# A gated mix of two linear attentions on one core: the output weights' splitting copies get one place in each half iteration, behind the copies of K and V

## The chip, the cores and the metric

The kernel runs on one core of a Trainium2 chip. The metric is the device time of one execution in microseconds (us); the median of three runs counts. A profile of one execution gives the times of single instructions.

## The reference

Two attention blocks A and B work on the same input x of 2048 tokens by 448 features, with 16 heads of 28, and a gate mixes their outputs. Each block projects x to q, k and v, sends q and k through a matrix per head and through two softmaxes (of the result and of its negative), and attends linearly: a sum of phi_k^T V over all tokens, read by phi_q and divided by a denominator. All of it is fp32.

```python
def block(x, wqkv, w_phi, wo):                 # once for A, once for B
    qkv = (x @ wqkv).reshape(B, S, 3, H, Dh).transpose(2, 0, 3, 1, 4)
    q, k, v = qkv[0], qkv[1], qkv[2]
    pq = einsum("bhsd,hdf->bhsf", q, w_phi)
    pk = einsum("bhsd,hdf->bhsf", k, w_phi)
    phi_q = concatenate([softmax(pq), softmax(-pq)], -1)
    phi_k = concatenate([softmax(pk), softmax(-pk)], -1)
    kv = einsum("bhsf,bhsd->bhfd", phi_k, v)
    z = einsum("bhsf->bhf", phi_k)
    num = einsum("bhqf,bhfd->bhqd", phi_q, kv)
    den = einsum("bhqf,bhf->bhq", phi_q, z)[..., None] + 1e-6
    return (num / den).transpose(0, 2, 1, 3).reshape(B, S, D) @ wo
g = sigmoid((x * gate_w).sum(-1, keepdims=True))
out = g * block_A(x) + (1 - g) * block_B(x)
```

## The kernel before

**Tiles.** The 2048 tokens are 16 tiles of 128. Each tile has three projections on TensorE: K and Q (weights already multiplied with the feature matrices, in `rk` and `rq`) and V (`rv`). Every fp32 operand is split in two: a *high part* (a copy to the rounded type fp32r, on ScalarE, `ACT`) and a *low part* (the rest, a subtraction on GpSimd, `POOL`, or VectorE, `DVE`). A projection of a tile and block is then 11 matmuls into one PSUM bank: `K0`, `K1` for K, `Q`, and `VA`, `VB` or `O0` for V. Inside the main loop 10 of them come together, and the last ones of K, Q and V are gathered in `halves` (L449 in the profile).

**A half iteration.** The loop `for p in range(2, 6)` in `steps()` has two halves, i = 0 and 1, of about 13 to 14 us each. A half projects K of tile k, Q of tile q = k - 2 and V, and takes these results onward. ScalarE copies V out of its banks (rows `vs<-VA`, `vs<-VB`, `vs<-O`) and K out of its two (`pk<-K`, twice). VectorE takes maxima and minima of K (`mx`), GpSimd subtracts them, ScalarE makes the exponentials (`ret<-ret`), VectorE sums them (`sm`), and GpSimd normalises (`ret<-ret,sm`). Q goes the same way on a longer road: VectorE reads the bank (`qmx`, `ru`), a transfer to DRAM and back turns it (`qd<-ru`, then `ru<-qd`), and behind that come two more exponentials (`ret<-ru`, `ret<-ret 128x32x28`). At every second half, TensorE accumulates phi_k^T V of two tiles into bank `T0` (`kv`, L535).

**The output weights.** They come as 7 chunks of 128 rows. `wo_rows` brings them into the right row order in DRAM (`wos`). `split_wo(c)` does one chunk: a load into the staging buffer (`wst<-wos`, 224 KB), the high part on ScalarE, the low part on GpSimd, and a store of each (`wod<-wst`). There is one staging buffer: the load of a chunk can begin only when the low part of the chunk before has read it, and the high part's own buffer is free when its store is done. `load_wo` brings all chunks into `rk`, when the last K projection has read it (`rk<-wod`, twice 1.6 MB). The output projection uses them from about 248 us on (L672).

**What sets the order.** Each step is put in by `plan.add(engine, cost, function, reads, writes)` (`put` adds with a cost by size). Reads and writes are names such as `("ws", 0)`, the staging buffer, or `("pk", 0, b)`, the K copy of an even tile, and give the dependences. `Plan.order` then runs a list scheduler over the steps with these costs: TensorE keeps the order of `steps()`, on every other engine the ready step with the earliest due time goes first. Each engine executes its queue in the order that comes out, and waits for semaphores at the head of it.

`split_wo` is called from `steps()` by `"wo", c`: chunk 0 in the loop at p = 2, chunks 1 and 6 both at p = 3, i = 0, chunk 2 at p = 4, chunk 3 at p = 5, chunks 4 and 5 behind the loop. In the loop a list `behind` already exists, with the names of the copies of K and of V of this half; it is given to `S`, the first softmax part of Q, whose exponential so comes behind these copies.

Of the kernel before, what the change touches and what calls it, by code (L numbers as in the profile page):

```python
# [108 lines left out]
def steps():  # L109

    yield from (("V01", 0, 0, 1), ("x1",), ("V01", 1, 0), ("V01", 1, 1), ("wt", 0), ("wt", 1), ("x", 2), ("wt", 2), ("wt", 3), ("V", 2, 0), ("F", 0, "DP"), ("V", 2, 1))
    yield from (("V", 3, 0), ("F", 1, "NP"), ("V", 3, 1), ("F", 2, "DP"), ("V", 4, 0), ("F", 3, "DP"), ("x2",), ("later",), ("V", 4, 1), ("k", 0, 0), ("q", 0, 0), ("k", 0, 1), ("ks", 0))
    yield from (("K", 1), ("wo_rows",), ("q", 0, 1), ("qf", 0))
    yield from (("S", 0, JIT % 3 - 1), ("K", 2), ("Q", 1), ("S", 1, (JIT - 1) % 3 - 1), ("k", 3, 0), ("k", 3, 1), ("vm", 5, 0), ("kv", 0, 1), ("vo", 5, 0), ("ks", 3), ("V", 5, 1))
    for p in range(2, 6):
        yield "x", p + 1
        for i in range(2):
            k, q, v = 2 * p + i, 2 * p - 2 + i, 2 * p + 1 + i
            yield "k10", k
            yield "q10", q  # L120
            yield "halves", k, q, v if v >= 6 else None
            if i:
                yield "kv", q - 1, q
            yield "ks", k
            yield "qf", q
            if v >= 6:
                yield "vo", v, 0
                yield "vo", v, 1
            behind = [("pk", k % 2, b) for b in range(2)] + [("v", v % NV, b) for b in range(2) if v >= 6]
            if q > 2:  # L130
                yield "S", q - 1, (JIT - q + 1) % 3 - 1, behind
            if i == 0:
                yield "wo", p - 2
                if p == 3:
                    yield "wo", 6
            yield "v10" if k < 11 else "V", v + 1
    yield from (("x", 7), ("K", 12), ("S", 9, 0, [("pk", 0, b) for b in range(2)]), ("Q", 10), ("turn", JIT - 2, 1), ("turn", JIT - 1, 0), ("wo", 4), ("k", 13, 0), ("k", 13, 1), ("kv", 10, 11), ("ks", 13), ("Q", 11), ("gates", 0, 12), ("gates_b", 0, 12))
    yield from (("K", 14), ("V", 14, 0), ("k", 15, 0), ("k", 15, 1), ("kv", 12, 13), ("wo", 5), ("load_wo",), ("Q", 12), ("ks", 15), ("V", 14, 1), ("V", 15, 0), ("q", 13, 0), ("q", 13, 1))
    yield from (("V", 15, 1), ("free_v",), ("free_k",), ("kv", 14, 15), ("free_e",), ("fetch", 0, 2), ("fetch", 1, 3))
    yield from (("kv_turn",), ("gates", 12, NT), ("qf", 13), ("Q", 14))  # L140
    kept, late = list(range(2, JIT - 2)), list(range(JIT, NT))
    rest = []
    while kept or late:
        rest.append((kept.pop(0) if kept else late.pop(0), late.pop(0) if late else kept.pop(0)))
    pairs = [((JIT - 1, JIT - 2), (0, 1)), ((0, 1), (2, 3))] + [(t, (2 * (i % 2), 2 * (i % 2) + 1)) for i, t in enumerate(rest)]
    for p, (tiles, slots) in enumerate(pairs):
        yield "num", tiles, slots
        if p == 0:
            yield from (("Q", 15), ("free_x",), ("free_q",))
        if p:  # L150
            for i, t in enumerate(pairs[p - 1][0]):
                yield "out", 2 * p - 2 + i, t, ("O0", "O1")[i]
        end = p == len(pairs) - 1
        yield "mix", p, ("DVE", "DVE") if end else ("POOL", "POOL"), ("T0", "T1"), ("DVE", "DVE") if end else ("POOL", "POOL")
        if p == 1:
            yield "gates_b", 12, NT, [("o", 2)]
        if p + 2 < len(pairs):
            for t, s in zip(*pairs[p + 2]):
                yield ("S" if t >= JIT else "fetch"), t, s, *([[("qd", 14, 3)]] if t == 2 else [[("ob", 0)]] if t == 3 else [])
    for i, t in enumerate(pairs[-1][0]):  # L160
        yield "out", 2 * len(pairs) - 2 + i, t, ("O0", "O1")[i]


JIT = 10
# [4 lines left out]
def hedgehog_mix(ctx: ExitStack, tc: tile.TileContext, xd, wv, wkt, wqt, wphi, wo, cmask, cpmask, out):  # L169
# [106 lines left out]
    def put(eng, n, fn, r, w, **k):  # L276
        add(eng, both(eng, n), fn, r, w, **k)
# [120 lines left out]
                add("SP", 0.4, dma(wos[:, i:i + n, c].rearrange("g i n -> i g n"), r[lo - DH * k:lo - DH * k + n]), [("q", "l", 1, 1, 2)], [("wos", c, i)], lat=3, kb=16 * n)  # L398
                lo += n

    def split_wo(c):
        s = [wst[:, i] for i in range(3)]
        f = [wst.bitcast(F32R)[:, i] for i in range(3)]
        add("SP", 0.4, dma(s[0], wos[:, :, c].rearrange("g i n -> (g i) n")), [k for k in plan.writer if k[:2] == ("wos", c)], [("ws", 0)], lat=2.4, kb=229)
        put("ACT", D, act(f[1], s[0]), [("ws", 0)], [("ws", 1)])
        put("POOL", D, tt("POOL", f[2], s[0], s[1], OP.subtract), [("ws", 0), ("ws", 1)], [("ws", 2)])
        for i in range(2):
            add("SP", 0.4, dma(wod[i][:, c], s[1 + i]), [("ws", 1 + i)], [("wod", i, c)], lat=2, kb=229)
# [327 lines left out]
    for what, *a in steps():  # L736
# [16 lines left out]
        elif what == "q":  # L753
            q_proj(*a)
        elif what == "qf":
            q_front(*a)
        elif what in ("k10", "q10", "v10"):
            for b in range(2):
                {"k": k_proj, "q": q_proj, "v": v_proj}[what[0]](*a, b, True)
        elif what == "halves":  # L760
            halves(*a)
        elif what == "Q":
            for b in range(2):
                q_proj(a[0], b)
            q_front(a[0])
        elif what == "turn":
            q_turn(*a)
        elif what == "S":
            q_soft(*a)
            if a[0] in SPILL:  # L770
                spill(*a[:2])
        elif what == "F":
            fold(*a)
        elif what == "kv":
            kv_acc(a)
        elif what == "x":
            load_x(a[0])
            if a[0] == 2:
                split_x(2, 0, P, "DVE")
            else:  # L780
                split_x(a[0], 0, 2 * P, "POOL")
        elif what == "x2":
            split_x(2, P, 2 * P, "DVE", after=[("k", "h", 1, 0, 2)])
        elif what == "x1":
            for i in range(2):
                split_x(1, i * P, i * P + P, ("DVE", "POOL")[i])
            plan.hand_over([("x0raw", i) for i in range(2)], [("xraw",), ("xraw", "b")])
            plan.hand_over([("x0" + k, i) for k in "hl" for i in range(4) if (k, i) != ("l", 3)], [(k, 0, i) for k in ("x", "xl") for i in range(2)])
        elif what == "wt":
            if a[0] == 2:  # L790
                plan.hand_over([("wvr", c, b) for c in range(4) for b in range(2)], wt1)
            load_wt(*a)
        elif what == "wo":
            split_wo(a[0])
        elif what == "num":
            p = nums[0]
            nums[0] += 1
            tiles = a[0]
            ctv = num(p, tiles, a[1])
            loaded[p] = tiles, ctv  # L800
        elif what == "mix":
            tiles, ctv = loaded[a[0]]
            for i, t in enumerate(tiles):
                n = outs[0] + i
                mix(a[0], i, t, n, ctv, a[1][i])
                o_turn(n, a[2][i], a[3][i])
            outs[0] += len(tiles)
        elif what == "out":
            out_mm(*a)
        elif what == "fetch":  # L810
            fetch(*a)
        elif what == "gates":
# [56 lines left out]
```

## Time and profile before

| what | value |
|---|---|
| runs, us | 341.45, 338.61, 341.44; median 341.44 |
| the profiled execution, us | 340.36 |
| its span, first to last instruction, us | 338.6 |
| mean granted clock of TensorE | 0.993 |
| TensorE busy | 329.7 us, 97% |
| VectorE busy | 281.4 us, 83% |
| GpSimd busy | 251.1 us, 74% |
| ScalarE busy | 147.1 us, 43% |
| moved by DMA | 54.74 MB, mean 162 GB/s |

The span is shorter than the profiled execution's time by 1.76 us, which lie before the first and behind the last instruction. Busy shares are means over stages with different limits; what a step is worth shows in the rows of its own stage. In the rows, PE is TensorE, PEld its weight loads, ACT ScalarE, POOL GpSimd, DVE VectorE, SP SyncE (which issues nearly all DMAs); `x<-y` is what an instruction writes and reads, without buffer numbers; `L267` is the line of the helper for all ScalarE activations, `L264` that for two-operand operations, `L270` that for DMAs.

### The profile page before, as it was taken

How to read it: one execution, taken by the hardware profiler on the slowest of the kernel's cores; microseconds unless marked ns; L12 is line 12 of the kernel's file. 1: busy time of each engine (PE TensorE's matmuls, PEld its weight loads, DVE VectorE, ACT ScalarE, POOL GpSimd, SP SyncE). 2: the span in 40 equal slices, each digit the busy share in tenths (PEclk: the TensorE clock that was granted, in tenths of full speed). 3: DMA queues.
4: the chain of work that ended last, by engine and by line, in shares of the span. 5: the costliest groups of instructions: out<-in, count | busy, mean ns of one | idle time of the engine just before them, and what ended most of it. 6: DMA issues, size and time to landing. Idle time of an engine off the chain costs nothing.

```text
span 338.6 us, 8905 instructions
## 1 busy us (share of the span) xinstructions
PE 329.7 (97%) x3742; PEld 291.9 (86%) x3742; DVE 281.4 (83%) x339; ACT 147.1 (43%) x244; POOL 251.1 (74%) x210
## 2 busy tenths in 40 slices
PE   8999999999999998699999999999999999999995
PEld 7977999998898897689899999999888888788894
DVE  4547979798878896779799999887899999999960
ACT  4747845451625542636428253522052442533231
POOL 7218769989899898999878999864179768888400
PEclk9999999999999999799999999999999999999999
DMA  7872046523573848577362532575876445141011
GB/s 252 244 234 73 0 148 191 158 98 88 200 246 124 266 111 291 172 257 220 147 218 63 178 111 55 214 277 171 243 237 219 170 170 186 72 168 56 32 55 54
DMA packets 29872, 54.74 MB, mean 162 GB/s; under 512 B 4632, under 2 KB 25480, under 8 KB 27528
## 3 DMA queue, kind: packets, MB, share of 16 engines
q1 hardware_dynamic: 29576, 54.06, 48.8%
q8 instruction: 29, 0.48, 0.6%
q0 software_dynamic: 256, 0.12, 0.1%
q14 instruction: 11, 0.09, 0.1%
HBM read 31.54 MB, written 24.22 MB: 165 GB/s over the span
## 4 chain that ended last, share of the span: by engine, by line
PE 50%; DVE 22%; POOL 16%; issue 5%; DMA 4%; ACT 2%; SPq 0%; POOLq 0%; DVEq 0%; ACTq 0%
PE O L672 10%; PE Q L424 10%; POOL ret L264 9%; PE K L424 9%; PE VB L424 6%; DVE ret L586 3%; DVE rv L635 3%; DVE sm L523 3%; POOL rv L644 3%; PE VA L424 3%; PE T L535 3%; PE N L624 2%; PE O L424 2%; DMA wst<-wos 2%; POOL rx L264 2%
## 5 line engine op out<-in xcount | busy, mean ns | idle before, releaser
L672 PE MATMUL O<-rk,rx 128*128 128x448 f32 x336 | 70.6, 368 | 0.1
L672 PEld LDWEIGHTS O<-rk,rx 128*128 128x128 f32 x336 | 62.5, 188 | 8.5 <-ACT rx L663 1.2
L424 PE MATMUL K<-rk,rx 128*128 128x432 f32 x336 | 69.4, 362 | 0.0
L424 PE MATMUL Q<-rq,rx 128*128 128x432 f32 x336 | 69.3, 360 | 0.0
L267 ACT ACTIVATE ret<-ret 128x896 f32<-128x896 f32 x48 | 45.7, 955 | 53.2 <-POOL ret L264 53.1
L424 PEld LDWEIGHTS K<-rk,rx 128*128 128x128 f32 x336 | 64.0, 190 | 3.1
L424 PEld LDWEIGHTS Q<-rq,rx 128*128 128x128 f32 x336 | 62.9, 188 | 3.5 <-DVE ru L264 0.4
L264 POOL TENSOR_TENSOR ret<-ret,sm 128x896 f32<-128x896 f32 x32 | 54.0, 1704 | 14.0 <-DVE sm L524 12.9
L523 DVE TENSOR_REDUCE sm<-ret 128x32 f32<-128x896 f32 x32 | 34.0, 1069 | 7.7 <-ACT ret L267 7.7
L586 DVE STREAM_TRANSPOSE ret<-ret 128x2048 f32<-128x2048 f32 x16 | 36.6, 2290 | 1.7 <-POOL ret L264 1.5
L424 PE MATMUL VB<-rv,rx 128*128 128x448 f32 x147 | 33.3, 375 | 3.7 <-ACT vs L267 3.7
L576 DVE TENSOR_REDUCE qsm<-ret 128x32 f32<-128x896 f32 x32 | 33.1, 1056 | 2.4 <-ACT ret L267 2.1
L424 PEld LDWEIGHTS VB<-rv,rx 128*128 128x128 f32 x147 | 27.7, 191 | 7.6 <-ACT vs L267 4.1
L264 POOL TENSOR_TENSOR ret<-qmn,ru 128x896 f32<-128x896 f32 x16 | 28.2, 1763 | 4.2 <-DVE ret L586 4.2
L264 POOL TENSOR_TENSOR ret<-pk,mx 128x896 f32<-128x896 f32 x16 | 27.3, 1706 | 4.7 <-DVE mx L516 4.7
L267 ACT ACTIVATE ret<-ru 128x896 f32<-128x896 f32 x16 | 15.5, 966 | 29.9 <-issue 17.3
L264 POOL TENSOR_TENSOR ret<-ret,qsm 128x896 f32<-128x896 f32 x16 | 27.3, 1704 | 0.9
L264 POOL TENSOR_TENSOR ret<-mx,pk 128x896 f32<-128x896 f32 x16 | 27.3, 1706 | 0.7 <-DVE mx L517 0.7
L644 POOL TENSOR_TENSOR rv<-rv,rd 128x896 f32<-128x896 f32 x14 | 23.9, 1704 | 1.1
L550 DVE TENSOR_REDUCE qmx<-Q 128x32 f32<-128x896 f32 x16 | 17.2, 1078 | 7.8 <-PE Q L449 4.3
L267 ACT ACTIVATE pk<-K 128x448 f32<-128x448 f32 x32 | 16.4, 543 | 14.3 <-PE K L424 11.5
L624 PE MATMUL N<-ret,kvt 32*32 32x256 f32 x1024 | 22.1, 385 | 0.0
(106 smaller groups left out, 487.2 us busy)
## 6 DMA issues: line engine op xcount, KB each, us to landing
ed<-ret SPq DMA_DIRECT2D x8, 1024.0 KB
ret<-ed SPq DMA_DIRECT2D x8, 1024.0 KB
qd<-ru SPq DMA_DIRECT2D x64, 112.0 KB
ru<-qd SPq DMA_DIRECT2D x16, 448.0 KB
out<-ret SPq DMA_DIRECT2D x16, 224.0 KB
wod<-wst SPq DMA_DIRECT2D x14, 224.0 KB
rk<-wod SPq DMA_DIRECT2D x2, 1568.0 KB
xraw<-in_xt SPq DMA_DIRECT2D x5, 512.0 KB
```

What stands on the lines that cost most here:

```text
L264: return lambda: ENG[eng].tensor_tensor(val(o), val(a), val(b), op)
L267: return lambda: A.activation(val(o), val(i), f, **k)
L424: nc.tensor.matmul(bank[name][:, k, lo:hi], x[:, xc, o:o + P], w[l][:, c], start=i == 0, stop=i == len(terms) - 1 and not part)
L523: put("DVE", 2 * D, lambda s=s, e3=e3: V.tensor_reduce(sm[:, s], e3, AX.X, OP.add), [ke[s], *([("u", 0, 1)] if t == 15 else [])], [("sm", ...
L535: nc.tensor.matmul(kvp()[32 * r:32 * r + DH + 1, b, g], vs[t % NV][:, b, h // 2, h % 2], es[t % NE][:, :, hs:hs + DH], start=(t == 0 and b ...
L550: put("DVE", 2 * D, lambda: V.tensor_reduce(mx, p4(), AX.X, OP.max), ["Q"], [km])
L576: put("DVE", 2 * D, lambda s=s, e3=e3: V.tensor_reduce(qsm[:, s], e3, AX.X, OP.add), [ke[s], *late], [("qsm", i, s)])
L586: add("DVE", 2.25, lambda: V.transpose(eTf[slot], eqs[j].rearrange("p s a c f -> p (s a c f)")), turned(j - 1) + [("u", 0, 1)] * (k == JIT ...
L624: nc.tensor.matmul(bank["N"][32 * g:32 * g + 32, r, 2 * b * P:2 * b * P + 2 * P], kvt[32 * r:32 * r + 32, b, s, g], eTp[slots[0] // 2][32 ...
L635: add("DVE", 0.07 + 1.08 * nt, lambda: V.transpose(ctr().rearrange("p (r n) -> p r n", r=4), bank["N"][:, :, :2 * nt * P]), ["N"], [("ctr" ...
L644: put(eng, 2 * D, lambda: ENG[eng].tensor_tensor(mid["o", n % 3].rearrange("p (c a f) -> p a c f", c=4, a=8), ctv()[:, :, i, :, :DH], rd[: ...
L672: nc.tensor.matmul(bank[pb][:, 0, :D], a, w, start=i == 0, stop=i == len(terms) - 1)
```

## The change

The high part of a chunk now names `behind` among its reads, so that it comes after the copies of K and V of its half iteration. Chunk 6, which was put in together with chunk 1, is put in one half later (p = 3, i = 1). Chunk 4, behind the loop, waits for the copies of K of tile 12; chunk 5 has no such list.

```diff
--- before
+++ after
@@ steps(), at the end of each half
             behind = [("pk", k % 2, b) for b in range(2)] + [("v", v % NV, b) for b in range(2) if v >= 6]
             if q > 2:
                 yield "S", q - 1, (JIT - q + 1) % 3 - 1, behind
-            if i == 0:
-                yield "wo", p - 2
-                if p == 3:
-                    yield "wo", 6
+            if i == 0 or p == 3:
+                yield "wo", 6 if i else p - 2, behind
@@ behind the loop
-    ... ("turn", JIT - 1, 0), ("wo", 4), ("k", 13, 0), ...
+    ... ("turn", JIT - 1, 0), ("wo", 4, [("pk", 0, b) for b in range(2)]), ("k", 13, 0), ...
@@ split_wo
-    def split_wo(c):
+    def split_wo(c, behind=()):
-        put("ACT", D, act(f[1], s[0]), [("ws", 0)], [("ws", 1)])
+        put("ACT", D, act(f[1], s[0]), [("ws", 0), *behind], [("ws", 1)])
@@ the caller
-            split_wo(a[0])
+            split_wo(*a)
```

TensorE's order is the same in both kernels. The other engines' orders change, since the scheduler runs anew. Three places matter.

The first is ScalarE's queue in the middle of the loop (p = 4). Before, from the exponential of a Q tile to the V and K copies of the next half:

```order
L267 ACTIVATE ret<-ru 128x32x28
L267 ACTIVATE ret<-ret 128x32x28
L267 ACTIVATE rx<-xraw 64x256
L267 ACTIVATE ret<-ret 128x896
L267 ACTIVATE wst<-wst 128x448
L267 ACTIVATE ret<-ret 128x896
L267 ACTIVATE wst<-wst 128x448
L267 ACTIVATE vs_74<-VB 128x16x28
L267 ACTIVATE pk_68<-K_97 128x448
L267 ACTIVATE pk_68<-K_98 128x448
```

The same stretch now, and on to the next chunk:

```order
L265 ACTIVATE ret<-ru 128x32x28
L265 ACTIVATE wst<-wst 128x448
L265 ACTIVATE ret<-ret 128x32x28
L265 ACTIVATE rx<-xraw 64x256
L265 ACTIVATE ret<-ret 128x896 x2
L265 ACTIVATE vs_74<-VB 128x16x28
L265 ACTIVATE pk_68<-K_97 128x448
L265 ACTIVATE pk_68<-K_98 128x448
L265 ACTIVATE vs_74<-O_555 128x16x28
L265 ACTIVATE glog<-O_555 128x1
L265 ACTIVATE ret<-ru 128x32x28
L265 ACTIVATE wst<-wst 128x448
```

Of the two high parts between the K exponentials, one has gone ahead of the Q exponential that waits for GpSimd, and the other has gone behind the V and K copies of the half that follows.

The second place is GpSimd's queue over the same time. Before:

```order
L264 TENSOR_TENSOR ret<-qmn_88,ru 128x32x28
L264 TENSOR_TENSOR wst<-wst 128x448
L264 TENSOR_TENSOR rx<-xraw,rx 64x256
L264 TENSOR_TENSOR rx<-xraw,rx 128x768
L264 TENSOR_TENSOR ret<-pk_69,mx_83 128x896
L264 TENSOR_TENSOR ret<-mx_83,pk_69 128x896
L264 TENSOR_TENSOR wst<-wst 128x448
L264 TENSOR_TENSOR ret<-ret,sm_85 128x896 x2
L264 TENSOR_TENSOR qsm_90<-qsm_90 128x32
L264 TENSOR_TENSOR ret<-ret,qsm_90 128x32x28
L264 TENSOR_TENSOR ret<-qmn_89,ru 128x32x28
L264 TENSOR_TENSOR wst<-wst 128x448
```

And now:

```order
L262 TENSOR_TENSOR ret<-qmn_88,ru 128x32x28
L262 TENSOR_TENSOR rx<-xraw,rx 64x256
L262 TENSOR_TENSOR rx<-xraw,rx 128x768
L262 TENSOR_TENSOR ret<-pk_69,mx_83 128x896
L262 TENSOR_TENSOR ret<-mx_83,pk_69 128x896
L262 TENSOR_TENSOR wst<-wst 128x448
L262 TENSOR_TENSOR ret<-ret,sm_85 128x896 x2
L262 TENSOR_TENSOR qsm_90<-qsm_90 128x32
L262 TENSOR_TENSOR ret<-ret,qsm_90 128x32x28
L262 TENSOR_TENSOR ret<-qmn_89,ru 128x32x28
L262 TENSOR_TENSOR ret<-pk_68,mx_82 128x896
```

Three low parts become one: those behind the two subtractions of Q's minima are gone from here.

The third place is behind the loop, ScalarE's queue around tiles 13 and 14, where the last chunk now stands. Before:

```order
L267 ACTIVATE ret<-ret 128x32x28
L267 ACTIVATE ret<-ret 128x896 x2
L267 ACTIVATE pk_68<-K_97 128x448
L267 ACTIVATE pk_68<-K_98 128x448
L267 ACTIVATE vs_74<-VA 128x16x28
```

And now:

```order
L265 ACTIVATE ret<-ret 128x32x28
L265 ACTIVATE ret<-ret 128x896
L265 ACTIVATE wst<-wst 128x448
L265 ACTIVATE ret<-ret 128x896
L265 ACTIVATE pk_68<-K_97 128x448
L265 ACTIVATE pk_68<-K_98 128x448
```

The last high part stands between the two exponentials of tile 13, ahead of the copies of K of tile 14; before, all chunks were through long before this place. On SyncE the store of the last low part stands between the two loads of `rk` in consequence, where before the two loads stood together.

More of the change, by code (lines that the diff above doesn't have):

```diff
@@ L131, in steps @@
                 yield "S", q - 1, (JIT - q + 1) % 3 - 1, behind
-            if i == 0:
-                yield "wo", p - 2
-                if p == 3:
-                    yield "wo", 6
+            if i == 0 or p == 3:
+                yield "wo", 6 if i else p - 2, behind
             yield "v10" if k < 11 else "V", v + 1
-    yield from (("x", 7), ("K", 12), ("S", 9, 0, [("pk", 0, b) for b in range(2)]), ("Q", 10), ("turn", JIT - 2, 1), ("turn", JIT - 1, 0), ("wo", 4), ("k", 13, 0), ("k", 13, 1), ("kv", 10, 11), ("ks", 13), ("Q", 11), ("gates", 0, 12), ("gates_b", 0, 12))
+    yield from (("x", 7), ("K", 12), ("S", 9, 0, [("pk", 0, b) for b in range(2)]), ("Q", 10), ("turn", JIT - 2, 1), ("turn", JIT - 1, 0), ("wo", 4, [("pk", 0, b) for b in range(2)]), ("k", 13, 0), ("k", 13, 1), ("kv", 10, 11), ("ks", 13), ("Q", 11), ("gates", 0, 12), ("gates_b", 0, 12))
     yield from (("K", 14), ("V", 14, 0), ("k", 15, 0), ("k", 15, 1), ("kv", 12, 13), ("wo", 5), ("load_wo",), ("Q", 12), ("ks", 15), ("V", 14, 1), ("V", 15, 0), ("q", 13, 0), ("q", 13, 1))
```

## The prediction

> **What bounds the kernel now.** I read the page first: how busy each engine is along the span (40 slices of 8.5 us), and under it the clock that TensorE was granted, in tenths.
>
> ```profile
> PE   8999999999999998699999999999999999999995
> PEclk9999999999999999799999999999999999999999
> ```
>
> TensorE has no holes except one, near slice 16, and the clock dips at the same place. The table of waits, asked for TensorE alone, names it: who waited for whom, us in total, times, longest.
>
> ```profile
> PE VB L424 <- ACT vs L267: 3.7, 1, 3.7
> ```
>
> One wait of 3.7 us, for ScalarE's copy of a V tile out of bank VB. The chain of waits says why that copy was late (start, duration, what):
>
> ```profile
> 130.24 1.12 POOL wst L264
> 131.38 5.74 DMA wst<-wos
> 138.28 3.06 PE VB L424 x10
> 141.35 4.72 PE K L424 x20
> ...
> 154.78 2.03 PE VB L424 x10
> 156.80 3.93 PE K L424 x20
> ```
>
> A low part of the output weights ends on GpSimd, only then the next chunk may be loaded into the one staging buffer (wst<-wos, 5.74 us), and after that load come TensorE's VB matmuls, which have nothing to do with it. ScalarE's rows in order of time show the reason (idle before, with its releaser, in brackets):
>
> ```profile
> 129.47 0.56 ACT L267 ACTIVATE wst<-wst 128x448 fp32r<-128x448 f32 x1
> 130.28 0.95 ACT L267 ACTIVATE ret<-ret 128x896 f32<-128x896 f32 x1 [0.24 <-POOL ret L264]
> 137.22 0.58 ACT L267 ACTIVATE wst<-wst 128x448 fp32r<-128x448 f32 x1 [6.00 <-DMA wst<-wos]
> 137.71 0.53 ACT L267 ACTIVATE vs<-VB 128x448 f32<-128x448 f32 x1
> ```
>
> Two high parts stand in this half iteration. The second waits 6.00 us for its load, and the V copy stands behind it in ScalarE's queue; it runs right after. TensorE's own rows show what that holds up:
>
> ```profile
> 131.43 0.47 PE L449 MATMUL VB<-rv,rx 64*128 64x448 f32 x1
> 138.28 3.06 PE L424 MATMUL VB<-rv,rx 128*128 128x448 f32 x10 [3.74 <-ACT vs L267]
> ```
>
> The matmul whose result is copied began at 131.43 and was over near 131.9. TensorE goes on with VA, is through at 134.55 (138.28 - 3.74) and needs bank VB. And it pays once more after the gap (window, width, busy times by engine, granted clock, DMA share, GB/s):
>
> ```profile
> 139.50:141.00 1.50, 1.50 (x6) 1.33 (x5) 1.50 (x2) 1.50 (x4) 1.50 (x3) 0.52 0.86 233
> 141.00:142.00 1.00, 1.00 (x4) 0.91 (x4) 1.00 (x2) 0.27 (x1) 1.00 (x1) 0.50 0.30 70
> 142.00:143.00 1.00, 1.00 (x5) 0.92 (x4) 1.00 (x1) 0.39 (x1) 1.00 (x2) 0.52 0.82 222
> ```
>
> From 139.5 to 143.0 the granted clock is 0.50 to 0.52. In the chain the ten VB matmuls take 3.06 us there against 2.03 one half iteration later, the twenty K matmuls 4.72 against 3.93: 1.03 + 0.79 = 1.82 us.
>
> So the event costs **3.74 + 1.82 = 5.56 us** of TensorE time. On either side TensorE is without a gap and each half iteration costs what its matmuls cost.
>
> **The change, part by part.** It removes and adds no instruction of work; seven high parts (0.56 to 0.61 us) and seven low parts get other places. I put the new places on the clock of before by their neighbours in the order.
>
> *High parts.* The group of them, with shortest, median and longest in ns and the first and last start:
>
> ```profile
> L267 ACT ACTIVATE wst<-wst x7: 561/578/607, 54.2 to 154.9; 128x448 fp32r<-128x448 f32 x7
> ```
>
> Two of the seven, at 129.5 and 137.2, stood in one half iteration. They now come at about 78, 107, 121, 140, 168, 190 and 203. The wait that the change adds is on ScalarE's own copies of K and V, which stand ahead of the high part in the same queue, and costs nothing by itself. No two share a half iteration, and none stands between the second exponential and the V copy. The stalled one (now the third, at 121) is through long before 131.9, so the V copy runs there. **Gain: 5.56 us**, all of it on the path that sets the end, since TensorE is the engine that has no other gap.
>
> What is late next? The fourth high part now follows V, pk, pk, V and one exponential, which with the V copy at 132.0 puts ScalarE there at about 135.0. Its load is issued when the third low part ends. For the bounds of a load I have two rows besides the 5.74 us of the chain:
>
> ```profile
> 140.95 0.34 SPq L270 DMA_DIRECT2D wst<-wos  x1
> 143.74 0.58 ACT L267 ACTIVATE wst<-wst 128x448 fp32r<-128x448 f32 x1 [0.17 <-DMA wst<-wos]
> ```
>
> Issued at 140.95, waited for until 143.74: 2.79 us. The third low part ends at 130.18 + 1.18 - 1.16 = 130.2 (one low part less ahead of it), so the load is there between 133.0 and 135.9, and ScalarE waits at most 0.9 us. What is queued behind it shows in one row of GpSimd and one of ScalarE:
>
> ```profile
> 138.04 1.77 POOL L264 TENSOR_TENSOR ret<-qmn,ru 128x896 f32<-128x896 f32 x1
> 150.46 0.55 ACT L267 ACTIVATE vs<-VB 128x448 f32<-128x448 f32 x1 [5.23 <-PE VB L449]
> ```
>
> The exponential behind it takes what GpSimd delivers at 138.04 + 1.77 - 1.16 = 138.65, so the wait is covered; the next V copy is due at 150.46 - 5.56 = 144.9. The wait that stopped TensorE is turned into one under which nothing is due. **Cost 0**; if the cover were gone, 0.9.
>
> *Low parts on GpSimd.* Its rows:
>
> ```profile
> 123.00 1.16 POOL L264 TENSOR_TENSOR wst<-wst 128x448 fp32r<-128x448 f32 x1
> 159.05 1.15 POOL L264 TENSOR_TENSOR wst<-wst 128x448 fp32r<-128x448 f32 x1
> 225.82 3.37 POOL L264 TENSOR_TENSOR ret<-ret,sm 128x896 f32<-128x896 f32 x2 [3.31 <-DVE sm L524]
> ```
>
> The wst rows at 123.0 and 159.05 leave their places, and one between them: three by 1.16, 3.48 us less GpSimd work before 165. In exchange one comes at about 172, one at 200 (where the gate row was) and one at 215. GpSimd has room there: in the last row here it idled 3.31 us for VectorE. SyncE issues the same 14 stores and 7 loads, each behind the step that it waits for; the place that could matter is the last, below.
>
> *Does the rest follow 5.56 us earlier?* VectorE's rows answer, at the maxima and minima that open each half iteration:
>
> ```profile
> 139.13 1.09 DVE L516 TENSOR_REDUCE mx<-pk 128x32 f32<-128x896 f32 x1 [2.33 <-ACT pk L267]
> 150.87 1.09 DVE L550 TENSOR_REDUCE qmx<-Q 128x32 f32<-128x896 f32 x1 [1.62 <-PE Q L449]
> 165.52 1.09 DVE L550 TENSOR_REDUCE qmx<-Q 128x32 f32<-128x896 f32 x1 [2.33 <-PE Q L449]
> 221.15 1.09 DVE L550 TENSOR_REDUCE qmx<-Q 128x32 f32<-128x896 f32 x1 [1.78 <-PE Q L424]
> ```
>
> VectorE stood 2.33 us in the stall itself, then waited 1.62 and 2.33 us for TensorE: 6.28 us of slack by 165, more than 5.56. So it is back in step with TensorE within two half iterations, from its own idle time. GpSimd gets 3.48 us by work that left, and needs its idle time for the rest. The next deadline is the last kv accumulation, which needs GpSimd's last normalisation:
>
> ```profile
> 204.22 0.95 ACT L267 ACTIVATE ret<-ret 128x896 f32<-128x896 f32 x1 [0.70 <-POOL ret L264]
> 206.24 0.55 ACT L267 ACTIVATE pk<-K 128x448 f32<-128x448 f32 x1 [1.06 <-PE K L424]
> 210.40 4.49 PE L424 MATMUL K<-rk,rx 128*128 128x432 f32 x22
> 232.07 1.78 PE L535 MATMUL T<-ret,vs 128*29 128x56 f32 x128
> ```
>
> GpSimd's last normalisation ends at 225.82 + 3.37 = 229.19, 2.88 us before its accumulation, and began only when VectorE let it, which in turn waited 1.78 us for TensorE (221.15). These waits move along with TensorE. **Cost 0, bounded by 2.1 us** (5.56 - 3.48), if none of GpSimd's idle time can be used.
>
> *The last chunk.* Its high part now stands just ahead of the exponential at 204.22, with the copies of K behind. Its load goes out when the low part of the chunk before ends: that begins behind this row:
>
> ```profile
> 198.36 1.70 POOL L264 TENSOR_TENSOR ret<-ret,sm 128x896 f32<-128x896 f32 x1
> ```
>
> It ends at 200.06, and on a GpSimd by then 3.5 to 4 us early the low part ends at 197.2 to 197.7; the load arrives 2.79 to 5.74 us later, at 200.0 to 203.4. The bank whose copy stands at 206.24 is needed by the K matmuls at 210.40 - 5.56 = 204.84. High part 0.58, exponential 0.95 and copy 0.55 before it make 2.08 us, so the load may land up to 202.8: **0 to 0.6 us**. I take 0.2, nearer the short end, because the transfers there are fewer than where the load took 5.74 us (the second row; the last two columns are DMA share and GB/s):
>
> ```profile
> 197.00:202.00 5.00, 5.00 (x145) 4.51 (x145) 4.97 (x6) 2.17 (x3) 4.44 (x4) 1.00 0.64 183
> 131.00:134.50 3.50, 3.50 (x19) 2.43 (x17) 2.74 (x5) 0.23 (x1) 2.11 (x3) 1.00 0.95 375
> ```
>
> The chunk's low part, at about 211, is stored, and the second load of rk waits for it; before, both were issued by 215.73.
>
> ```profile
> 214.92 0.81 SPq L270 DMA_DIRECT2D rk<-wod  x2
> 248.19 9.02 PE L672 MATMUL O<-rk,rx 128*128 128x448 f32 x42
> ```
>
> The first output matmul that needs rk would stand at 242.6. From 211 plus one store and one load of 1.6 MB, at the 375 GB/s of the row above 4.3 us, it is there by about 222: covered by 20 us.
>
> *Sum.* 340.36 (the profiled execution: 338.6 of span and 1.76 around it) - 5.56 + 0.2 = **335.0 us**. The profiled execution lies 1.1 us under the median of the three runs, 341.44, and inside their range, so against the median the step is 6.4 us or 1.9%. About 1% (3.4 us) is what a measurement of this kernel can tell from no change; under 338.03 counts as faster.
>
> *A page against the row.* On the 1.82 us, the Trainium skill's page "TensorE: Matmul & The Clock Gate", in Part 1 under "What's actually happening", says that an idle window of about 3.4 us halves the matmul clock and that a busy one of that length restores it, with windows that run on their own. The trace agrees: 3.74 us idle, then 3.5 us at 0.50 to 0.52. By that rule the half clock goes away with the gap and the sum stands; if the dip had a cause of its own and stayed, the sum would be 336.8.
>
> **The rivals.** *A: VectorE and GpSimd become the bound.* Both were near full around the stall. Then only what leaves them is gained: 2.33 us on VectorE (the wait at 139.13) or 3.48 us on GpSimd, 336.9 to 338.0. For it: the chain stands on GpSimd, not on TensorE, at 130.24. Against it: the 1.62, 2.33 and 1.78 us that VectorE waits for TensorE.
>
> *B: the stall moves instead of going.* A high part still waits for its load in ScalarE's queue, and if another thing late on GpSimd makes the V copy late, 3.74 us idle and the half clock come back at another half iteration: 340.4. For it: one staging buffer, so every load still waits for a low part. Against it: behind each new place stand exponentials that wait for GpSimd anyway.
>
> *C: slower, by the last chunk.* If its load lands L us after 197.5, TensorE waits L - 5.3 us for the K copy, and where that is as long as the gap of now, the slow clock's 1.82 us come on top. All of the gain is eaten from L = 9.1 on (3.8 idle and 1.82 behind it); at L = 13.5 the time is about 344.8, 1% over the median. Against it: 2.79 and 5.74 are what such loads took, the longer one in full traffic.
>
> That the change does not do what it says is excluded for the order, since the rows show the moved places; what remains of that is B.
>
> **How the numbers follow.** Forecast 335.0: 0.60. A: 0.18, of which I give 0.14 to times under 338.03. B: 0.14, counted as the same. C and its like: 0.08. That gives faster 0.74, same 0.18, slower 0.08. The low end is 333.0, the forecast without its 0.2 and with 1.8 us for the spread of runs (338.61 lies 1.75 below 340.36); the high end, 339.5, takes in A, the 336.8 and part of B. Outside stay C, half of B and 0.04 below.
>
> **What would show it.** In the profile after: no row of waits of TensorE on the V copy, and a clock of 1.00 in every window of the loop; a high part that waits for its load with the exponential behind it, not the V copy; VectorE's maxima no longer waiting 2.33 us for pk; O matmuls starting about 5.4 us earlier. The prediction is wrong if TensorE's idle time in the loop exceeds about 2 us anywhere, or if VectorE and GpSimd delay the start of N.

## The result, and the profile after

| | before | after |
|---|---|---|
| median of four runs, us | 340.25 (338.61 to 341.45) | **335.03** (334.76 to 336.65) |
| ratio to before, with its 95% interval | | 0.9854 [0.9807, 0.9902] |
| the profiled execution, us | 340.36 | 336.65 |
| its span, us; clock | 338.6; 0.993 | 334.9; 1.000 |

The change is worth 5.2 us or 1.5%. Here and below, the ratios leave out three executions that were over 1.5% above the fastest of their kernel: 343.44 us (kernel before), 342.99 us (ten matmuls added) and 533.58 us (18 matmuls added, mean clock 0.561).

In the page, TensorE's row and the clock's row have lost the place near slice 16:

```profile
PE   8999999999999999999999999999999999999995
PEclk9999999999999999999999999999999999999999
```

In the table of waits of TensorE no row names the V copy. Behind the first 66 us one row is left (N are the matmuls that read the sums out for phi_q):

```profile
PE N L622 <- PE Q L422: 0.3, 1, 0.3
```

ScalarE's rows around the old hole (start, duration, what; in brackets the idle time ahead and what ended it):

```profile
122.36 0.61 ACT L265 ACTIVATE wst<-wst 128x448 fp32r<-128x448 f32 x1
129.41 0.96 ACT L265 ACTIVATE ret<-ret 128x896 f32<-128x896 f32 x1 [0.71 <-POOL ret L262]
133.47 0.55 ACT L265 ACTIVATE vs<-VB 128x448 f32<-128x448 f32 x1 [3.10 <-PE VB L447]
136.38 0.56 ACT L265 ACTIVATE wst<-wst 128x448 fp32r<-128x448 f32 x1
```

The high parts of this stretch start at 122.4 and, behind the copies, at 136.4. Neither waits, and none stands between the second exponential (129.41) and the V copy. The V copy now waits for TensorE (3.10 us), where before TensorE waited for it. In the chain the two groups that had run at half clock have their usual times (before: 3.06 and 4.72), and the windows over the old dip have a clock of 1.00:

```profile
136.07 2.03 PE VB L422 x10
138.10 3.93 PE K L422 x20
```

```profile
139.50:141.00 1.50, 1.50 (x9) 1.43 (x9) 1.17 (x2) 0.96 (x1) 1.50 (x2) 1.00 0.44 100
141.00:142.00 1.00, 1.00 (x7) 0.95 (x6) 0.96 (x2) 0.55 (x1) 1.00 (x2) 1.00 0.73 176
142.00:143.00 1.00, 1.00 (x7) 0.95 (x6) 1.00 (x2) 0.40 (x1) 1.00 (x2) 1.00 1.06 418
```

**Where the 3.7 us between the spans come from.** The spans differ by less than the 5.56 us of the forecast, since the profiled executions do not reach the loop at the same time. The first accumulation of phi_k^T V (T), before which no high part lies on TensorE's way, started here (before; after; after in the second profile below):

```profile
64.37 1.78 PE L535 MATMUL T<-ret,vs 128*29 128x56 f32 x128
65.90 1.78 PE L533 MATMUL T<-ret,vs 128*29 128x56 f32 x128
64.82 1.78 PE L533 MATMUL T<-ret,vs 128*29 128x56 f32 x128
```

From there to the end of the span it is 338.6 - 64.37 = 274.2 us before, and 334.9 - 65.90 = 269.0 after: **5.2 us** less. I call this stretch the *body*. The start of the body moves by over 1 us between two executions of one kernel, so it is the body that shows what an edit does, and the table at the end of the experiments goes by it.

### The profile page after: what moved, and what is told of

The parts are those of the page before. It is cut to its first block, busy times and chain, and to the rows that moved or that the text cites. A ratio compares the mean times of both kernels' runs of the same rounds, so it can differ in the third digit from the quotient of the medians.

```text
span 334.9 us, 8903 instructions
## 1 busy us (share of the span) xinstructions
PE 328.8 (98%) x3742; PEld 291.1 (87%) x3742; DVE 282.2 (84%) x339; ACT 147.0 (44%) x244; POOL 251.2 (75%) x210
## 4 chain that ended last, share of the span: by engine, by line
PE 67%; DVE 10%; DMA 8%; POOL 7%; SPq 4%; issue 2%; ACT 1%; POOLq 0%; ACTq 0%
PE K L422 19%; PE Q L422 17%; PE O L670 10%; PE VB L422 7%; PE VA L422 4%; PE T L533 4%; SPq L268 4%; PE O L422 3%; POOL rv L642 3%; DMA qd<-ru 3%; DVE rv L633 3%; DMA ret<-in_xt 3%; DVE ret L584 2%; PE N L622 2%; POOL ret L262 2%
## 5 line engine op out<-in xcount | busy, mean ns | idle before, releaser
L422 PEld LDWEIGHTS K<-rk,rx 128*128 128x128 f32 x336 | 63.0, 188 | 3.8 <-DVE rk L262 0.9
L422 PE MATMUL VB<-rv,rx 128*128 128x448 f32 x147 | 32.5, 367 | 0.0
L265 ACT ACTIVATE vs<-VB 128x448 f32<-128x448 f32 x15 | 8.2, 545 | 32.5 <-PE VB L447 22.0
```

What stands on the lines that cost most here:

```text
L265: return lambda: A.activation(val(o), val(i), f, **k)
L422: nc.tensor.matmul(bank[name][:, k, lo:hi], x[:, xc, o:o + P], w[l][:, c], start=i == 0, stop=i == len(terms) - 1 and not part)
```

## The experiments

Theory: the whole gain is one place in ScalarE's queue, where a high part that waits for its load stood ahead of the V copy; TensorE's idle time behind it also brings the half clock. Rivals: the new places of the low parts on GpSimd bring it; the spread to one chunk each half brings it; the half clock has a cause of its own.

In the kernels with a moved row or with added matmuls the scheduler's order is kept as found and single steps are taken to another place in their engine's queue. On engines that are not named, the order is row by row that of the kernel they start from. (The spread alone, chunk 6 one half later and no `behind`, gives the order of the kernel before on every engine, so there was nothing to run.)

```diff
     def emit(self):
-        for i in self.order()[0]:
+        queues = ...                     # each engine's steps in the order found
+        for what, after in MOVES:        # take step `what` to behind step `after`
+            ...
```

### One row moved in the kernel before

```diff
+MOVES = (("high", 3), ("qexp", 5)),     # ACT: the stalled high part to behind the exponential of Q
```

> The kernel before with one row moved: on ScalarE the second high part of the half iteration with the hole stands behind the copies of V and K and the query's exp, and no longer ahead of the V copy; GpSimd, VectorE, the DMA queue and TensorE keep their order row by row. Theory (the whole gain is this one place in ScalarE's queue): no gap of TensorE at 134.6 to 138.3 and no half clock behind it, so 5.56 us less than the kernel before, 334.8 to 335.3; the high part still waits about 0.7 us for its load (there at about 137.1, the query's exp ends at about 136.5). Rival, that the earlier low parts on GpSimd and what they do to VectorE bring it: within 1 us of the kernel before, 339.5 to 341. Rival, that the half clock has a cause of its own: 3.74 us less and the half clock still there, 336.5 to 337.

Measured: **334.72 us** (334.39 to 336.88), ratio 0.9869 [0.9800, 0.9938]. ScalarE's and TensorE's rows:

```profile
133.93 0.55 ACT L283 ACTIVATE vs<-VB 128x448 f32<-128x448 f32 x1 [1.27 <-PE VB L467]
137.57 0.58 ACT L283 ACTIVATE wst<-wst 128x448 fp32r<-128x448 f32 x1 [0.18 <-POOL ret L280]
136.38 2.19 PE L442 MATMUL VB<-rv,rx 128*128 128x448 f32 x10
```

The V copy waits for TensorE again, and VB follows without a gap. GpSimd's low parts and the loads stand where they stood, and the gain is complete. The moved high part waits 0.18 us. Beside the changed kernel on one chip:

> The kernel before with the one row of ScalarE moved, beside the changed kernel on one chip. Theory (this row is the whole of the change's gain): the two medians within 0.7 us of each other. Rival (the spread of the other high parts and the earlier low parts carry part of it): the changed kernel at least 1 us faster.

> The changed kernel, unchanged, on the same chip as the next two, to compare with: 334.8 to 336.0.

Measured: 335.71 us (334.73 to 336.53) with the one row, 335.38 (335.11 to 337.15) for the changed kernel; 0.33 apart. The rivals on the low parts and the spread fall.

### The spread taken away

```diff
-            if i == 0 or p == 3:
-                yield "wo", 6 if i else p - 2, behind
+            if i == 0:
+                yield "wo", p - 2, behind
+                if p == 3:
+                    yield "wo", 6, behind
```

> The changed kernel with chunk 6 called in the same half iteration as chunk 1, as before the change; the high parts still stand behind their half's copies of K and V. The planner orders anew: the high part of the third chunk in the loop stands right ahead of the V copy at 118.8, but its load goes out at about 111.4 and is there by 115 to 117. Theory: no stall of more than a few tenths, 334.8 to 335.5, as the changed kernel. Rival, that the spread to one chunk each half is what gains: 339 to 341.

Measured: 335.74 us (335.12 to 336.47), ratio 0.9890 [0.9814, 0.9966]. The load of the third high part was issued at 111.30, it had no wait at 114.84, and the V copy behind it waited 1.49 us for TensorE. What this kernel has more than the changed one is a longer wait at N (the last row; 0.28 and 0 us there):

```profile
114.84 0.58 ACT L267 ACTIVATE wst<-wst 128x448 fp32r<-128x448 f32 x1
116.91 0.55 ACT L267 ACTIVATE vs<-VB 128x448 f32<-128x448 f32 x1 [1.49 <-PE VB L449]
131.57 0.55 ACT L267 ACTIVATE vs<-VB 128x448 f32<-128x448 f32 x1 [2.47 <-PE VB L449]
134.17 0.61 ACT L267 ACTIVATE wst<-wst 128x448 fp32r<-128x448 f32 x1
233.36 2.75 PE L624 MATMUL N<-ret,kvt 32*32 32x256 f32 x128 [0.88 <-PE Q L424]
```

So chunk 6 in a half iteration of its own is not needed either; the names in `behind` do it alone. The third high part stands ahead of a V copy in the kernel before too (115.79, its load issued at 112.38) and costs nothing in either kernel, since its load is there. What has changed is where the two stand that shared the half iteration with the hole: the fourth comes behind the copies, and the fifth, at 161.80, behind those of the half iteration after the next.

### A second staging buffer in the kernel before

```diff
-        add("SP", ..., dma(s[0], wos[...]), ..., [("ws", 0)])
-        put("ACT", D, act(f[1], s[0]), [("ws", 0)], [("ws", 1)])
+        raw, kr = (kvt, ...) if odd else (s[0], [("ws", 0)])    # kvt is not in use yet
+        add("SP", ..., dma(raw, wos[...]), ..., kr)
+        put("ACT", D, act(f[1], raw), kr, [("ws", 1)])
```

> The kernel before with a second buffer for the raw chunk (every other chunk is loaded into room that is free then), so that a load no longer waits for the low part ahead of it; the calls stay as before the change, and two high parts of one half iteration still stand ahead of the V copy. Theory (the wait for the load behind the low part made the hole): no hole, 334.7 to 336. Rival, that a high part ahead of the V copy costs whatever its load does: 338 to 340.

Measured: 336.46 us (335.74 to 336.90), ratio 0.9853 [0.9803, 0.9902].

```profile
131.77 0.58 ACT L267 ACTIVATE wst<-kvt 128x448 fp32r<-128x448 f32 x1 [0.15 <-POOL wst L264]
132.25 0.53 ACT L267 ACTIVATE vs<-VB 128x448 f32<-128x448 f32 x1
194.80 4.57 PE L430 MATMUL Q<-rq,rx 128*128 128x432 f32 x22 [1.50 <-DVE ru L264]
```

The second high part of the half iteration stands right ahead of the V copy, as before the change, and waits 0.15 us instead of 6.00. There is no hole. The median is 0.5 us above the expected range. The 1.50 us wait in the last row, for VectorE, is new: the scheduler ordered VectorE anew as well. Why it comes stays open.

### A high part put back ahead of the V copy, with a short and a long wait

```diff
 # in the changed kernel; the short wait has the first move, the long wait both
+MOVES = ((("high", 2), ("exp", 7, 1)),   # ACT: ahead of the V copy
+         (("low", 6), ("norm", 7, 1)))   # POOL: the low part that its load waits for, one row later
```

> The changed kernel with one row moved on ScalarE: the high part that stands at 136.38 in its trace goes ahead of the V copy of 133.47; all else keeps its order. Its load is issued at 130.5 after the low part of 129.33 and lands 3.7 to 5.7 us later, at 134.2 to 136.3, so the V copy ends at 135.2 to 137.3, while the next VB matmul is due at 136.07. Theory (what counts is how late the V copy gets, not that a high part stands ahead of it; the half clock needs a long gap): a gap of 0 to 1.3 us and no half clock, 335.0 to 336.5. Rival, that a high part ahead of the V copy costs what it cost before: about 340. Rival, that any gap brings the half clock: up to 338.

Measured: 337.03 us (335.88 to 339.01), ratio 0.9919 [0.9884, 0.9954].

```profile
129.64 0.32 SPq L284 DMA_DIRECT2D wst<-wos  x1
134.94 0.58 ACT L281 ACTIVATE wst<-wst 128x448 fp32r<-128x448 f32 x1 [5.46 <-DMA wst<-wos]
136.01 2.30 PE L440 MATMUL VB<-rv,rx 128*128 128x448 f32 x10 [2.05 <-ACT vs L281]
```

The gap is 2.05 us, above the 0 to 1.3 expected. The load took 134.94 - 129.64 = 5.3 us from its issue, inside the bounds, but TensorE reached the body 2.1 us earlier than in the first profile of the changed kernel (63.77 against 65.90), while the low part came only 0.9 us earlier (128.45 against 129.33): the expectation had taken TensorE's time from one execution. The clock is 1.00 behind the gap:

```profile
137.00:140.00 3.00, 3.00 (x17) 2.83 (x16) 3.00 (x3) 2.24 (x5) 2.19 (x3) 1.00 0.66 173
140.00:143.00 3.00, 3.00 (x17) 2.87 (x16) 2.97 (x4) 1.67 (x2) 2.85 (x3) 1.00 0.77 302
```

So in this profile the stall costs what it takes. The median is 2.0 us over the changed kernel's 335.03 (on another chip) and 2.3 us over the kernel with one row moved on this chip. Two of the ten runs have a mean clock of 0.992 and 0.995, and of them no profile is kept.

> As the kernel before this one, and the low part of 129.33 on GpSimd goes behind the second normalisation of keys (132.67 to 134.37) as well, so that the load is issued at about 135.6 and lands at 139.3 to 141.3: the V copy ends at 140.3 to 142.3 against the 136.07 at which VB is due. Theory: a gap of 4.2 to 6.3 us, followed by a half clock that costs about 1.8 us more, 341.0 to 343.1. Rival, that the half clock in the kernel before has a cause other than the gap: the gap alone, 339.2 to 341.3, with the clock at 1.00 behind it. Rival, that it was the low parts' times on GpSimd that made the difference (they move here by one row only): 335 to 336.

Measured: **341.75 us** (340.37 to 343.27), slower than the kernel before: 1.0061 [1.0024, 1.0099].

```profile
134.28 0.32 SPq L284 DMA_DIRECT2D wst<-wos  x1
137.06 0.58 ACT L281 ACTIVATE wst<-wst 128x448 fp32r<-128x448 f32 x1 [7.93 <-DMA wst<-wos]
138.12 3.78 PE L440 MATMUL VB<-rv,rx 128*128 128x448 f32 x10 [3.53 <-ACT vs L281]
137.00:140.00 3.00, 1.88 (x5) 1.71 (x6) 1.03 (x2) 2.94 (x7) 0.95 (x1) 0.66 0.74 230
140.00:143.00 3.00, 3.00 (x13) 2.74 (x13) 3.00 (x3) 2.06 (x3) 2.87 (x2) 0.77 0.50 153
```

A gap of 3.53 us (the load took 2.8 us this time, so it is below the 4.2 expected) and then a clock of 0.66 and 0.77 in three-microsecond windows. VB takes 3.78 us against the 2.30 of the row above. Putting one high part ahead of the V copy again, with a load that is late, brings the whole loss back.

### Work put into the hole

Is the half clock the price of idle time? Ten VA matmuls ahead of the hole are done twice (x4 in the kernel before, x5 in the kernel with the long gap), or 18 are added (x6). The first passes' results are overwritten.

```diff
 # v_proj, for tile 10 and block 0
-        add("PE", ..., mms(...), ...)
+        add("PE", ..., lambda: (mms(..., first 10)(), mms(...)()), ...)      # x4, x5
+        add("PE", ..., lambda: (mms(..., first 10)(), mms(..., first 8)(), mms(...)()), ...)   # x6
```

> The kernel before in its own order on every engine, and the ten VA matmuls that stand just ahead of the hole are done twice (the second pass starts the bank anew, so the values stay): 2.03 us of work that nobody needs, put into the 3.74 us of idle time. The hole for VB stays as long as it was, TensorE idles 1.7 us of it. Theory (a long idle stretch of TensorE is what brings the half clock behind it, about 1.8 us; 2.05 us of idle time brought none in the kernel with the short delay): the clock stays at 0.998 to 1.00 and the time falls by 1.0 to 1.8 us though work was added, from 340.0 to 338.2 to 339.0. Rival, that the half clock has a cause of its own: no change, 339.7 to 340.3, and the clock at 0.993.

Measured: 340.32 us (337.46 to 342.99) against 341.70 for the kernel before on that chip, ratio 0.9973 [0.9938, 1.0007]. The interval does not tell the two apart, although 2.03 us of work were added. The expected clock came in half of the runs only: of the twelve runs six have a clock of 1.00 (median 339.2) and six 0.992 to 0.995 (341.5); of the kernel before, 3 of 23 have 1.00 there.

In the profiled one VA is doubled, the gap is what is left, and VB runs at its usual pace:

```profile
132.67 4.38 PE L442 MATMUL VA<-rv,rx 128*128 128x450 f32 x20
139.04 2.28 PE L442 MATMUL VB<-rv,rx 128*128 128x448 f32 x10 [1.99 <-ACT vs L283]
```

> The kernel with the long delay (341.75 us, the clock at 0.988 to 0.995) with the same doubled VA matmuls inside the gap: of 3.5 to 5 us of idle time 1.5 to 3 are left. Theory: the half clock goes, 1.3 to 1.8 us less, 339.9 to 340.5, the clock at 0.998 to 1.00. Rival (the half clock has a cause of its own): 341.5 to 342.

Measured: 340.64 us (339.27 to 342.52) against 341.75 without the filling (on another chip, where the kernel before took 340.0 and not 341.7). That is 0.1 us above the expected range. Eight of twelve runs have 0.997 or more, of the ten without filling none. The profiled one fell among the four others and shows something new (VA doubled, then VB, and the clock behind it):

```profile
132.59 4.38 PE L440 MATMUL VA<-rv,rx 128*128 128x450 f32 x20
139.41 3.76 PE L440 MATMUL VB<-rv,rx 128*128 128x448 f32 x10 [2.44 <-ACT vs L281]
140.00:143.00 3.00, 3.00 (x10) 2.69 (x9) 2.75 (x3) 2.40 (x5) 1.58 (x1) 0.50 0.52 174
```

An idle time of 2.44 us was enough here for a clock of 0.50.

> The kernel before in its own order, with eighteen VA matmuls more (3.65 us of work that nobody needs) inside the hole of 3.74 us, so that TensorE idles 0.1 us of it. With ten of them (1.99 us idle in the profiled run) half the runs kept a clock of 1.00 (median 339.2 us) and half had 0.992 to 0.995 (median 341.5). Theory (the half clock comes from idle time in the hole, and less of it makes it rarer): nearly every run at 0.997 to 1.00, 338.5 to 340 us, 1.5 to 3 us under the kernel before of the same chip, although TensorE does 3.65 us more. Rival, that the clock has a cause besides: as many runs at 0.988 to 0.995 as before, and no change or up to 0.5 us slower.

Measured: 340.1 us (338.16 to 340.60), against 341.33 for the kernel before on that chip: 0.9954 [0.9930, 0.9977]. **All eleven runs that count have a clock of 0.997 to 1.00**, while all 17 of the kernel before have 0.988 to 0.995. TensorE does 3.65 us more and the kernel is 1.2 us faster; 1.5 to 3 were expected. (It is still 4.7 us slower than the changed kernel on that chip.) A mean of 0.997 needs no dip in the loop: in one profile below (all chunks in the loop, second time) it has this value, and the clock falls only behind the last matmul. The hole was longer in this profile (VB waited 1.60 us more, behind 28 matmuls):

```profile
131.88 6.01 PE L442 MATMUL VA<-rv,rx 128*128 128x450 f32 x28
139.48 2.30 PE L442 MATMUL VB<-rv,rx 128*128 128x448 f32 x10 [1.60 <-ACT vs L283]
```

With the three together, the rival that the half clock has a cause of its own falls.

### All seven chunks inside the loop

```diff
-            if i == 0 or p == 3:
-                yield "wo", 6 if i else p - 2, behind
+            if k < 11:
+                yield "wo", k - 4, behind
 # and no "wo" behind the loop
```

> The changed kernel with all seven chunks inside the loop, one each half iteration, each high part behind the copies of K and V, and none behind the loop; the last load of the high rows then goes out earlier. Theory: the changed kernel's last small wait (0.28 us at N, behind the load of the second half of the output weights that is issued at 220.34) goes, and ScalarE's 2.02 us wait for the last chunk too: 334.5 to 335.0. Rival: three more low parts inside the loop crowd GpSimd and VectorE, and a V or K matmul waits: 335.5 to 337.

Measured: 335.41 us (334.57 to 336.04), ratio 0.9821 [0.9780, 0.9862], on a chip where the kernel before took 341.70. That is 0.4 us above the expected range. No wait of TensorE behind the first 66 us, and the two loads of the output weights go out together again:

```profile
209.40 0.91 SPq L268 DMA_DIRECT2D rk<-wod  x2
```

> All seven chunks in the loop, beside the changed kernel on one chip: 335.41 against 335.03 on different chips. Theory: the same as the changed kernel within 0.5 us, since what it removes (0.28 us at N) is less than the spread of the prologue from run to run (1.6 us); rival: faster by 0.3 us or more.

Measured: 334.41 us (334.27 to 334.42, four runs), 0.9807 [0.9776, 0.9838], beside 335.38 and 0.9850 [0.9819, 0.9881] for the changed kernel. The medians are 0.97 us apart, more than the 0.5 that the theory allowed, and all four runs lie below all six of the changed kernel. But the intervals of the ratios overlap, and the bodies below are 268.66 and 268.68 us, the same: in the profiles the 0.9 us lie ahead of the body (it starts at 63.94 and 64.82). It is the best median of all, and whether it is better than the changed kernel stays open; what is shown is that it removes the small wait at the end where that occurs.

### The bodies, added up

The body of the changed kernel in its second profile, in which TensorE waits nowhere behind T, is 268.7 us. Every other profile follows from it, to within 0.4 us, by the waits and the added work that its own rows show (waits of 0.2 us are left out):

| kernel | body, us | 268.7 and the rows |
|---|---|---|
| before | 274.2 | + 3.74 (gap) + 1.82 (half clock) = 274.3 |
| one row moved, twice | 268.7, 268.6 | |
| changed | 269.0 | + 0.28 (N) = 269.0 |
| spread taken away | 269.6 | + 0.88 (N) = 269.6 |
| second buffer | 270.3 | + 1.50 (Q) = 270.2 |
| short wait put back | 271.9 | + 2.05 (gap) + 0.8 (N) = 271.6 |
| long wait put back | 274.7 | + 3.53 (gap) + 1.75 (VB 3.78 for 2.03) + 0.7 (N) = 274.7 |
| before, ten VA matmuls added | 273.0 | + 2.06 (VA 4.38 for 2.32) + 1.99 (gap) = 272.8 |
| long wait, ten VA matmuls added | 275.6 | + 2.06 (added) + 2.44 (gap) + 1.73 (VB 3.76 for 2.03) + 0.3 (N) = 275.2 |
| before, 18 VA matmuls added | 274.7 | + 3.69 (VA 6.01 for 2.32) + 1.60 (gap) + 0.7 (Q) = 274.7 |
| all in the loop, twice | 268.9, 268.7 | |

The half clock rows (1.82, 1.75, 1.73) hold a part that any gap brings: right behind a gap VB takes 2.28 to 2.30 us at a clock of 1.00 (short wait, ten and 18 matmuls added), and 2.03 without one. Some 0.26 us of each are this, and about 1.5 us the clock.

## Why the prediction held, point by point

**The event, 5.56 us: right.** The body became 5.2 us shorter with a wait of 0.28 at N, so 5.5 us without it. The first output matmul stands 183.82 us behind the start of the body before and 178.59 after, 5.2 us earlier (5.4 predicted). Moving one row does the same. That the median came within 0.03 us of the forecast is luck: the profiled execution missed it by 1.65 us, because its body began 1.5 us later.

**The half clock goes with the gap: right; its size is that of one execution.** Over 59 runs of the kernel before that stood beside the experiments, on three chips, 7 had a clock of 0.997 or more (median 337.8 us), 30 had 0.992 to 0.995 (340.4) and 22 less (341.9). The order is the same within each chip. The 2.6 to 4.1 us between these need not all be the clock: a longer gap may bring the half clock more often. The page "TensorE: Matmul & The Clock Gate" of the Trainium skill (Part 1, "What's actually happening") gives an idle window of about 3.4 us as the condition, with windows that run on their own. The half clock did last that long, 3.4 us in each of the three profiles that have it (139.55 to 142.96 before, 137.95 to 141.37 with the long wait, 139.85 to 143.26 with ten matmuls added to it; from windows of 0.1 us). But 2.44 us of idle time were enough in the last of them, and 2.05 and 1.99 were not in two others. The measurement decides: a gap well under 3.4 us can bring it. An estimate from these times: if the clock falls at the end of a window as long as the half clock lasted, that window held 1.3 us of work in the kernel before, none with the long wait, and 1.0 us with the ten matmuls. That fits windows that count as idle with some work in them and whose place is chance; the threshold itself was not measured.

**Which high parts moved, and which way: told wrongly.** The prediction calls the third high part, at 121, the stalled one, and the section on the change lets one high part go ahead. The chunks keep their order, so the one that stalled is the fifth in both kernels, and all seven come later than before: the third at 122.36 (before 115.79, without a wait), the fourth at 136.38 (129.47), the fifth at 163.69 (137.22), with its load issued at 142.56, 21 us ahead. The gain did not hang on this: the sum needs only that no high part stands between the second exponential and the V copy.

**The fourth high part waits at most 0.9 us, covered: right.** It waited for nothing (136.38), since the load went out at 130.5 and ScalarE reached it only then.

**VectorE and GpSimd come back in step at no cost (rival A: 336.9 to 338.0): right.** VectorE's waits at the maxima of Q, 1.62 and 2.33 us before, are nearly used up:

```profile
161.49 1.09 DVE L548 TENSOR_REDUCE qmx<-Q 128x32 f32<-128x896 f32 x1 [0.80 <-PE Q L447]
158.72 3.36 POOL L262 TENSOR_TENSOR ret<-ret,sm 128x896 f32<-128x896 f32 x2 [2.51 <-DVE sm L522]
```

0.80 us of the second is left. So 3.15 of the two are gone, with the 2.33 us in the stall itself (at 139.13 before) 5.48 of the 5.56, and GpSimd still idles 2.51 us in between.

**The last chunk, 0 to 0.6 us, taken as 0.2: mis-sized, it was 0.** The load took 202.91 - 199.17 = 3.7 us, ScalarE waited 2.02 us for it, and the copies of K behind it were through by 205.2, ahead of the K matmuls:

```profile
199.17 0.36 SPq L268 DMA_DIRECT2D wst<-wos  x1
202.91 0.58 ACT L265 ACTIVATE wst<-wst 128x448 fp32r<-128x448 f32 x1 [2.02 <-DMA wst<-wos]
206.36 4.49 PE L422 MATMUL K<-rk,rx 128*128 128x432 f32 x22
```

**The second load of the output weights, covered by 20 us: the term that was mis-sized.** The matmuls that read it were covered. But it waits for a store that goes out at 214.35, was issued only at 220.34, and SyncE's queue stands behind it:

```profile
214.35 0.32 SPq L268 DMA_DIRECT2D wod<-wst  x1
220.34 0.32 SPq L268 DMA_DIRECT2D rk<-wod  x1
220.72 2.05 SPq L268 DMA_DIRECT2D qd<-ru  x4
232.70 1.09 DVE L568 TENSOR_REDUCE qmn<-ru 128x32 f32<-128x896 f32 x1 [1.67 <-DMA ru<-qd]
233.71 0.76 DVE L609 STREAM_TRANSPOSE kvt<-kvs 128x256 f32<-128x256 f32 x2
234.39 0.28 DVE L611 TENSOR_SCALAR kvt<-kvt 128x4 f32<-128x4 f32 x2
234.62 2.75 PE L622 MATMUL N<-ret,kvt 32*32 32x256 f32 x128 [0.28 <-PE Q L422]
```

The turning of Q (`qd<-ru`) came behind it, VectorE waited 1.67 us for its return and wrote `kvt` only then, and N, which reads `kvt`, waited 0.28 us. (The last row names Q's matmuls, but these had ended 0.28 us earlier.) Counted at 0, the load cost 0.28 in this profile and 0 in the next one (issued at 218.65; VectorE's wait was 0.75 us there). The prediction had looked at who reads the load, not at what is queued behind it. The place in the queue may not be all: without the spread the load went out at 217.54, the turning came 0.4 us behind it, and N waited 0.88 us; with both loads at 209.40 nothing waited. Whether the transfer of 1.6 MB itself slows the turning was not tested.

**B and C** did not occur: no stall of TensorE over 0.28 us is left in the body, and the load of the last chunk was far from the 9.1 us from which C decides. The experiment with the long wait is B made by hand: 341.75, where B was put at 340.4.

## What to carry to other kernels

When an engine at the bound waits, read which instruction stands ahead of its releaser in the releaser's queue: here a copy that nobody needed soon waited 6 us for a load, and a copy that TensorE needed at once stood behind it. Either order them the other way, or make the load early, and look at what a moved step's DMAs stand ahead of in the queue that issues them. Compare executions from a point behind the prologue, and add up the waits from there.

## What the runs showed that was not expected

- Useless work made the kernel before faster: 3.65 us of matmuls in a gap saved 1.2 us [0.9930, 0.9977], because the clock stayed at 0.997 to 1.00.
- 2.44 us of idle time of TensorE were followed by a clock of 0.50 for 3.4 us in one execution; after 2.05 and 1.99 us it stayed at 1.00 in two others. In 2 of 10 and 6 of 12 runs of these two kernels the mean clock was 0.992 to 0.995; how long their gaps were is not on record.
- From its issue until ScalarE could start, the same load of 224 KB took 2.8 us (long wait put back), 3.7 (the last chunk), 5.3 (short wait put back) and 5.8 us (before, 131.38 to 137.22).
- The start of the body varied from 63.7 to 66.4 us over 14 profiles, and from 64.82 to 65.90 for one kernel.
